# A convolution and softmax-feed-forward kernel: weights converted in PSUM tiles of their own, other load order, g on GpSimd, a second chunk of 16 tokens, four parts in groups 16 to 28

## The chip, the cores and the metric

The kernel runs on one core of a Trainium2 chip. The metric is the device time of one execution in microseconds, lower is better; the figure before is the median of three executions. The profile is of one further execution.

## The reference

Two steps, 8 x 4160 tokens of width 192. First a causal convolution with 7 taps whose weights are a softmax of their own for each token and each of 8 heads; then a feed-forward layer of width 1024 with an activation h * softmax(h), a layer norm over the 1024 values, and a second product.

```python
w = softmax(weight_gen, axis=-1)                      # (8, 4160, 8 heads, 7 taps)
a[b, s, h, :] = sum_k w[b, s, h, k] * x_pad[b, s + k, h, :]   # x_pad: 6 zeros before
h = a @ w_in                                          # (33280, 192) @ (192, 1024)
solu = h * softmax(h)
ln = (solu - mean) / sqrt(var + 1e-6) * g_ln
out = ln @ w_out                                      # (33280, 1024) @ (1024, 192)
```

`x`, `weight_gen` and `g_ln` arrive as float32, `w_in` and `w_out` as float64, and the kernel reads the latter as pairs of 32-bit words.

## The kernel before, in words

**Tiles and groups.** Each of the 128 partitions holds a run of 260 consecutive tokens, so "token t" is a tile of 128 rows, and there are 260 such tiles. x and the taps come in chunks that begin at tokens 0, 4, 12, 20, 36, ... (`starts`, L42). The tiles of x are two buffers (`xt`), used in turn. Within a chunk the convolution works in groups: of two tokens up to token 8, of four afterwards.

**One token.** For a group GpSimd makes the 7 products of x and taps (`attA`, L180), then adds them pairwise until a number of parts is left (`attB`, L195). With the flag True the parts are added by TensorE as it transposes them (`xT`, L474: three transposes of 128x128 for each part and each pair of tokens, accumulated in `pa`); with False VectorE adds them first (`fin`, L458) and one set of transposes follows. After token 16 the groups go through `PARTS`: 3 True, 2 False, 3 True, 3 False; `FIRST` overrules this for early groups. ScalarE and VectorE make a high and a low f16 half of it (`xhi` L484, `xld` L488), and a DMA swaps row halves (`sw`, L494). TensorE makes h in three f16 products (`mm1`, L508 and L513); odd tokens use a second copy of the weights whose rows are swapped (`w0`, `w1`, L290 to L294, DMAs). Then, for each h tile of 128x1024 in PSUM: VectorE scales it and takes its extreme (`max`, L525), ScalarE the exponential (`exp`, L531), VectorE the product (`solu`, L539), ScalarE the squares (`sq`, L545) and the high half (`hi`, L552), VectorE the low half (`lo`, L556), a transposing DMA turns both (`tr`, L564), TensorE makes the second product (`mm2`, L604), ScalarE scales it into `ot` (`out`, L615), and a DMA stores four tokens (`od`, L618). The layer norm's factors are made by small operations for 2 or 4 tokens together (`f0` to `f5`).

**Rings.** h has three PSUM buffers, `po` one. The three h buffers first serve as scratch for the weights, then tokens 0 to 3, then two tiles `c0` and `c1` of the centred second weights, then tokens 4, 5, ... So token 3 waits until token 0's `sq` and `lo` are done, and token 4 for those of token 3.

**The weights.** The words of a double are joined into a float32 by VectorE in PSUM (step 0: L256 once, L260 twice), ScalarE makes a square that tells tiny values (step 1: L266), VectorE multiplies (step 2: L270). `a0`, `a1` and `b` are the first weights, `c0` and `c1` the second. a0 and a1 share one scratch tile, b shares one with c0, c1 has one. The squares of the first weights are summed (`n0` to `n2`, L311), over partitions by TensorE (`n4`, L318), and give the factor `unit_w` (`n6` L322 to L325, `n7` L327), with which the f16 halves are made (`a03` and `a13` L334, `b3` L300 on ScalarE, `a04`, `a14` L336 and `b4` L302 on VectorE). The second weights, kept in the unused end of `xs[1]`, are multiplied by g on ScalarE, eight calls (`q00` to `q30`, L365), summed by TensorE (L370) and ScalarE (L375), centred (`p3`, L388) and split (`p7` L406, `p8` L411).

**Order.** The engines take their instructions in order. The order is made by `plan`, a list of steps with an engine, a cost and what each waits for, and by `issue_order`, which walks through them: the engine that is free takes, of the steps that are ready by the costs, the one with the lowest key. The key is the token's number plus an entry in the table `URGENCY`, by the step's name or by its name and token.

```python
        tile_of, first, n = key
        ...
            bits = bits_of[key] = scratch[tile_of][:, first : first + n].bitcast(I32)
```

Of the kernel before, what the change touches and what calls it, by code (L numbers as in the profile page):

```python
# [26 lines left out]
def tile_kernel(ctx: ExitStack, tc: tile.TileContext, x, weight_gen, w_in, w_out, g_ln, out):  # L27
    nc = tc.nc
# [13 lines left out]
    starts = [0, TG, TG + TC // 2, *range(TG + TC, RUN + 1, TC)]  # L42
# [204 lines left out]
    def float_of_double(key, raw, step, out=None):  # L247

        tile_of, first, n = key
        low = window(raw, 0, [(2, n)])  # L250
        high = window(raw, 1, [(2, n)])
        if step == 0:
            for which in range(len(scratch), 3):
                scratch[which] = ps_h.tile([P, FF], F32, name="h")
            bits = bits_of[key] = scratch[tile_of][:, first : first + n].bitcast(I32)
# [7 lines left out]
        elif step == 1:  # L263
            wide = n > FH
            size = size_of[key] = big.tile([P, n], F32, name="e" if wide else "size")
# [42 lines left out]
    def norm_of_first(step):  # L308
# [6 lines left out]
        elif step == 4:  # L315
            first["total"] = ps_o.tile([P, 512], F32, name="po")
# [34 lines left out]
    def convert(f, step):  # L351
        if step == 2 and "w2" not in second:
            second["w2"] = xs[1].rearrange("p (t d) -> p t d", d=D)[:, -NJ:]
        key = ((1, FH, FH), (2, 0, FF))[f]
        out = None
        if step == 2:
            out = second["w2"].rearrange("p j d -> p (j d)")[:, f * FH : f * FH + key[2]]
        float_of_double(key, raw[3 + f], step, out)
# [71 lines left out]
    def stat_group(t):  # L430

        n = 2 if t < 2 * TG else TG
        return n if t % n == n - 1 else 0
# [163 lines left out]
    def second_product(t):  # L597
        hlT = hlT_of.pop(t)

        free = t >= RUN - TG and t % 2 == 1  # L600
# [16 lines left out]
    def store(t):  # L617
        nc.sync.dma_start(o_run[:, t - TG + 1 : t + 1, :], o_of.pop(t // TG))  # L618
# [54 lines left out]
    a00=79.1, a01=227.6, a02=-179.6, a03=77, a04=-12.8, a10=2, a11=-93.6, a12=123.9, a13=124.9,  # L673
    a14=-132.6, attA=42.9, attA_0=-139.3, attA_2=38.7, attA_4=-121.9, attA_6=101.7, attA_8=-218.2,
    attB=39.9, attB_0=-162.5, attB_2=-4.3, attB_4=74.8, attB_6=-6.9, attB_8=38, b0=133.1, b1=124.8,
    b2=-185.2, b3=24.4, b4=6.5, c00=-95.6, c01=-188.7, c02=-219.3, c10=-222.3, c11=130.7, c12=-70.5,
    c20=-32.3, c21=-46.1, c22=-89, c30=95.7, c31=-78.4, c32=-191, dup=57.3, dup_0=0.9, dup_2=-49.2,
    dup_4=18.3, dup_6=109.3, dup_8=-102.8, exp=-62.2, exp_0=-133.3, exp_1=-123.8, exp_10=41,
    exp_11=-48.7, exp_2=130, exp_3=117.3, exp_4=-23.5, exp_5=-229.6, exp_6=143.2, exp_7=-6.5,
    exp_8=-204.3, exp_9=-18.4, f0=-44.8, f0_1=204, f0_11=72.8, f0_3=17.5, f0_5=17.9, f0_7=216.7,  # L680
    f1=-76, f1_1=20.8, f1_11=-49, f1_3=225.5, f1_5=239.7, f1_7=-14.9, f2=-157.8, f2_1=-115.4,
    f2_11=-19.4, f2_3=230.5, f2_5=-82.5, f2_7=-212.3, f3=34.7, f3_1=-22.7, f3_11=-9.5, f3_3=-53.7,
    f3_5=-121.9, f3_7=-4.3, f4=-58.5, f4_1=167.1, f4_11=69.9, f4_3=-149.7, f4_5=-211.4, f4_7=-100.7,
    f5=-113, f5_1=-19.9, f5_11=23.1, f5_3=75.1, f5_5=47.8, f5_7=96.3, fin=117.5, hi=-107.7,
    hi_0=83.5, hi_1=117.9, hi_10=-193.7, hi_11=86.1, hi_2=-36.8, hi_3=165.8, hi_4=-85.5, hi_5=32.6,
    hi_6=-10, hi_7=-26.8, hi_8=154.8, hi_9=166, lo=-80.2, lo_0=57.7, lo_1=-5.6, lo_10=102.5,
    lo_11=-17.3765, lo_2=-76.7, lo_3=23.7, lo_4=164.3, lo_5=95.8, lo_6=-169.7, lo_7=50, lo_8=-126.6,
    lo_9=75, lw=235.7, lx0=-56.1, lx1=92.4, lx2=8.2, lx3=54.9, max=202.4, max_0=-105.2, max_1=98.3,
    max_10=233.7, max_11=125.3, max_2=-23.8, max_3=200.8, max_4=-205, max_5=-32.1, max_6=149.3,
    max_7=-60.8, max_8=-133.6, max_9=-98.2, mm1=-25.2, mm1_0=-8.9, mm1_1=-9.6, mm1_10=239.3,  # L690
    mm1_11=96.5, mm1_2=158.9, mm1_3=48.1, mm1_4=130.2, mm1_5=-233.5, mm1_6=-5.2, mm1_7=-0.8,
    mm1_8=-2.4, mm1_9=50.4, mm2=-18.3, mm2_0=-4.1, mm2_1=-79.4, mm2_10=182.9, mm2_11=-132.6,
    mm2_2=-211.7, mm2_3=118.1, mm2_4=-93, mm2_5=-224.9, mm2_6=147, mm2_7=10.4, mm2_8=71.6,
    mm2_9=96.2, n0=-12.3, n1=122.3, n2=213.8, n3=-82.1, n4=-104.5, n5=-87.1, n6=-157.4, n7=-151.2,
    nq=-111.6, od=-89.4, od_11=20.6, od_3=16.1, od_7=25.3, out=-192.5, out_0=82.9, out_1=-156.2,
    out_10=54, out_11=-146.8, out_2=232.1, out_3=-56.4, out_4=-28.7, out_5=6.1, out_6=-127.6,
    out_7=23.7, out_8=-74.6, out_9=81.9, p30=-18.7, p31=-152.9, p4=235.2, p5=33.4, p6=-71.9,
    p70=197.2, p71=64.7, p80=-220.6, p81=-108.5, p9=116.9, q00=125.4, q01=-132, q02=161.9,
    q10=219.6, q11=-64, q12=-61.2, q20=206.5, q21=-15.5, q22=-201.1, q30=39.3, q31=0.6, q32=-134.4,
    solu=125.9, solu_0=20.8, solu_1=-3.5, solu_10=129.7, solu_11=17.6, solu_2=6.1, solu_3=-139.9,  # L700
    solu_4=-75.7, solu_5=-145.2, solu_6=161.6, solu_7=-195.9, solu_8=-29.1, solu_9=37.3, sq=-43.8,
# [12 lines left out]
    xld_10=99.8, xld_2=-77.8, xld_4=-238.1, xld_6=8.8, xld_8=133.1,
# [8 lines left out]
FIRST = {0: (7, True), 2: (7, True), 4: (5, True), 6: (5, True), 8: (4, True), 12: (4, True)}  # L723
# [3 lines left out]
def plan(run, starts, group, stat_group, loads, parts):  # L727
# [13 lines left out]
    weights = dict(a0=6600, a1=9300, b=10800, c0=13000, c1=16000)  # L741
    order = list(weights)
    for n, part in enumerate(order):
        at, wide = weights[part], part == "c1"
        once(part + "0", DVE, 3600 if wide else 2050, *([order[n - 1] + "0"] if n else []), ready=at)
        after = [order[n - 1] + "1"] if n else []
        once(part + "1", ACT, 1050 if wide else 620, *after, *([order[n - 2] + "2"] if n > 1 else []), ready=at)
        after = [part + "0", part + "1"]
        if n == 4:
            after.append(order[n - 1] + "2")  # L750
        once(part + "2", DVE, 1220 if wide else 700, *after)
# [6 lines left out]
    for f, part in enumerate(("c0", "c1", "c1", "c1")):  # L758
        once(f"q{f}0", ACT, 770, part + "2", ready=16000)
        once(f"q{f}1", PE, 660, f"q{f}0", *([f"q{f - 1}1"] if f else ["n6"]))  # L760
        once(f"q{f}2", ACT, 520, f"q{f}0", "c12", "n4")
# [25 lines left out]
    for c in range(len(starts) - 1):  # L787
        t, before = starts[c], starts[c - 1] if c > 1 else -1
        size = starts[c + 1] - t
        if c > 1:  # L790
            add("lw", t, SP, 1270, last_group(c - 3))
            add("lx0", t, SP, 1540, last_group(c - 2), *norms(c - 2), *([("p81", 0)] if c == 3 else []))
            for n in range(1, loads):
                add(f"lx{n}", t, SP, 1540, (f"lx{n - 1}", t))
        for n, (name, _) in enumerate(norms(c)):
            if c == 0:
                add(name, t, ACT, (1030, 1260)[n], ready=(7800, 6600)[n])
            else:
                load = [(f"lx{min(n + 1, loads - 1) if size == 16 else loads - 1}", t)] if c > 1 else []
                add(name, t, ACT, 840, *load, ready=18500 if c == 1 else 0)  # L800
# [239 lines left out]
```

## Time and profile before

| | |
|---|---|
| median of 3 executions | 1252.67 us (1252.61 to 1254.92) |
| the profiled execution | 1254.43 us, its span 1252.4 us |
| busy: PE / DVE / ACT / POOL | 1189.2 / 1157.0 / 1128.8 / 1145.7 us |
| instructions | 27,348 |

PE is TensorE, DVE is VectorE, ACT is ScalarE, POOL is GpSimd, SP issues the DMAs. An engine's time before an instruction stands in square brackets behind a row, with what ended it. PEclk is the clock granted to TensorE, as a share of its upper level of 2.4 GHz; 0.50 is its lower level, 1.2 GHz.

### The profile page before, as it was taken

To read this page: it belongs to the slowest core of one execution; us is meant where nothing else is said; L and a number is where in the kernel's file an instruction comes from. 1 tells how busy PE (TensorE), PEld (TensorE's weight loads), DVE (VectorE), ACT (ScalarE), POOL (GpSimd) and SP (SyncE) were. 2 spreads that over 40 slices of the span, in tenths; PEclk is the share of its full clock that TensorE was granted. 3 is DMA by queue.
4 is the path that set the end of the run, shared out by engine and by line. 5 is a ranking of instruction groups with operands and counts; after the bars stand their busy time and mean duration, and the time that the engine had idled before them with its cause. 6 is when DMAs were issued, how large, how long until landed. Compare 5 with 4: busy or idle time off the path is not lost.

```text
span 1252.4 us, 27348 instructions
## 1 busy us (share of the span) xinstructions
PE 1189.2 (95%) x10248; PEld 818.3 (65%) x10248; DVE 1157.0 (92%) x1786; ACT 1128.8 (90%) x2311; POOL 1145.7 (91%) x237
## 2 busy tenths in 40 slices
PE   2598899999999999999999999999999999999997
PEld 2365566666666666666666666666666666666666
DVE  6677999999999999999999999999999999999984
ACT  5778889898998989899998989999898989989886
POOL 5899999999999999999999999999999999999400
PEclk9799999999999999999999999999999999999999
DMA  7577688897989999798989989798988979877667
GB/s 222 112 189 172 132 190 168 192 197 144 213 169 198 176 183 199 149 213 165 212 166 181 184 170 213 152 208 166 202 164 191 199 145 198 167 148 149 139 140 139
DMA packets 586066, 219.75 MB, mean 175 GB/s; under 512 B 548687, under 2 KB 566223, under 8 KB 585806
## 3 DMA queue, kind: packets, MB, share of 16 engines
q1 hardware_dynamic: 585632, 216.91, 84.6%
q8 instruction: 80, 1.31, 0.4%
q10 hardware_dynamic: 302, 1.11, 0.3%
q14 instruction: 52, 0.43, 0.1%
HBM read 46.19 MB, written 25.56 MB: 57 GB/s over the span
## 4 chain that ended last, share of the span: by engine, by line
PE 34%; ACT 33%; DVE 17%; issue 11%; DMA 4%; SPq 0%; ACTq 0%; DVEq 0%
PE po L604 13%; PE h L513 11%; ACT e L531 9%; ACT e L545 8%; ACT hl L552 6%; PE h L508 6%; DVE h L539 5%; DVE h L525 4%; DVE a L458 4%; PE pa L474 3%; DVE hl L556 3%; ACT junk L145 3%; ACT ot L615 2%; DMA hlT<-hl 2%; ACT xh L484 2%
## 5 line engine op out<-in xcount | busy, mean ns | idle before, releaser
L180 POOL TENSOR_TENSOR pr<-xt,wt 128x5376 f32<-128x5376 f32 (+1 forms) x67 | 631.1, 9420 | 0.2
L604 PE MATMUL po<-w_hl,hlT 128*128 128x192 f16 x6192 | 554.1, 247 | 8.7 <-DMA hlT<-hl 4.5
L604 PEld LDWEIGHTS <-hlT 128*128 128x128 f16 x6240 | 523.1, 98 | 52.9 <-issue 6.0
L195 POOL TENSOR_TENSOR pr<-pr 128x2304 f32<-128x2304 f32 (+1 forms) x126 | 458.3, 3637 | 7.6
L556 DVE SCALAR_TENSOR_TENSOR hl<-h,hl 128x1024 f16<-128x1024 f32 x260 | 314.6, 1220 | 41.5 <-ACT e L545 26.4
L525 DVE TENSOR_SCALAR_CACHE_REDUCE h<-h,row 128x1024 f32<-128x1024 f32 x260 | 334.8, 1288 | 12.9 <-PE h L513 8.7
L539 DVE SCALAR_TENSOR_TENSOR h<-h,row,e 128x1024 f32<-128x1024 f32 x260 | 333.3, 1282 | 10.3 <-ACT e L531 7.6
L531 ACT ACTIVATE e<-h,stats 128x1024 f32<-128x1024 f32 x260 | 292.9, 1126 | 15.1 <-DVE h L525 14.4
L552 ACT ACTIVATE hl<-h 128x1024 f16<-128x1024 f32 x260 | 266.4, 1025 | 36.7 <-DVE h L539 18.5
L545 ACT ACTIVATE e<-h,stats 128x1024 f32<-128x1024 f32 x260 | 292.2, 1124 | 2.6 <-DVE h L539 2.0
L513 PEld LDWEIGHTS <-xh 128*128 128x128 f16 x1560 | 131.9, 98 | 236.5 <-issue 115.0
L513 PE MATMUL h<-w_odd,xh 128*128 128x512 f16 x780 | 192.7, 384 | 0.0
L513 PE MATMUL h<-wa_hi,xh 128*128 128x512 f16 x520 | 178.4, 384 | 0.0
L615 ACT ACTIVATE ot<-po,stats 128x192 f32<-128x192 f32 x258 | 110.5, 428 | 36.4 <-PE po L604 36.0
L508 PE MATMUL h<-w_odd,turned 64*128 64x512 f16 x390 | 107.4, 382 | 10.7 <-DVE hl L556 10.1
L508 PE MATMUL h<-wb_hi,xh 64*128 64x512 f16 x260 | 99.9, 384 | 14.6 <-DVE hl L556 12.5
L508 PE MATMUL h<-w_odd,xh 64*128 64x512 f16 x390 | 107.6, 383 | 0.0
L508 PE MATMUL h<-wb_hi,turned 64*128 64x512 f16 x260 | 100.1, 385 | 0.0
L513 PE MATMUL h<-wa_lo,xh 128*128 128x512 f16 x260 | 99.2, 381 | 0.0
L508 PEld LDWEIGHTS <-xh 64*128 64x128 f16 x780 | 54.7, 94 | 54.8 <-issue 26.0
L474 PE MATMUL pa<-ident,pr 128*128 128x128 f32 x678 | 87.7, 277 | 0.6 <-DVE xh L488 0.6
L474 PEld LDWEIGHTS pa<-ident,pr 128*128 128x128 f32 x678 | 78.6, 144 | 7.9 <-DVE xh L488 1.1
(89 smaller groups left out, 1020.4 us busy)
## 6 DMA issues: line engine op xcount, KB each, us to landing
out_dram<-ot SPq DMA_DIRECT2D x65, 384.0 KB, 3.5
xt<-in_x_dram SPq DMA_DIRECT2D x30, 576.0 KB, 5.0
xt<-in_x_dram SPq DMA_DIRECT2D x30, 480.0 KB, 4.3
turned<-xh SPq DMA_DIRECT2D x260, 32.0 KB, 2.6
wt<-in_weight_gen_dram SPq DMA_DIRECT2D x15, 448.0 KB, 4.8
hlT<-hl SPq DMA_TRANSPOSE x260, 4.6
xt<-in_x_dram SPq DMA_DIRECT2D x3, 384.0 KB, 4.4
pr<-in_moe_w_out_dram SPq DMA_DIRECT2D x1, 1024.0 KB, 10.3
```

The source lines that it names most:

```text
L180: nc.gpsimd.tensor_tensor(out=window(pr, 0, [(ROW, K), (HG, n * H), (1, HG)]), in0=window(xt, t * D, [(D, K), (HG, n * H), (1, HG)]), in1= ...
L195: nc.gpsimd.tensor_tensor(out=b, in0=b, in1=a, op=ALU.add)
L474: nc.tensor.matmul(pa[:, k], source[:, first : first + P], ident, is_transpose=True, start=at == 0, stop=at == 3 * len(sources) - 1,)
L508: nc.tensor.matmul(h[:, fs], last[(f + odd) % 2][rows, low], rhs[rows], start=n == 0, stop=False)
L513: nc.tensor.matmul(h[:, fs], xh[:, 2 * odd, low], rhs[:, fs], start=False, stop=n == 2)
L525: nc.vector.tensor_scalar(h, h, row(t, BACK), 3.0e38, op0=ALU.mult, op1=ALU.min, accum_out=stat(t, NMAX))
L531: nc.scalar.activation(e, h_of[t], AF.Exp, bias=stat(t, NMAX), scale=-1.0, accum_out=stat(t, Z))
L539: nc.vector.scalar_tensor_tensor(out=h, in0=h, scalar=row(t, SCALE), in1=e, op0=ALU.mult, op1=ALU.mult, accum_out=stat(t, M))
L545: nc.scalar.activation(e_of.pop(t), h_of[t], AF.Square, bias=stat(t, M), scale=-float(FF), accum_out=stat(t, Q),)
L552: nc.scalar.activation(hl[:, 0, :], h_of[t], AF.Copy, scale=2.0**14)
L556: nc.vector.scalar_tensor_tensor(out=hl[:, 1, :], in0=h_of[t], scalar=2.0**14, in1=hl[:, 0, :], op0=ALU.mult, op1=ALU.subtract,)
L604: nc.tensor.matmul(po[:, :D], hlT[:, half * NJ + j, :], w2_hl[:, j, w, :], start=n == 0, stop=n == len(terms) - 1,)
```

## The change

- The chunks begin at 0, 4, 20, 36, ...: one chunk of 16 tokens in place of two of 8. The second weights lie at the end of `xs[0]` now, whose next load, of the chunk at token 20, waits for them.
- x of the first chunk is loaded behind all of `w_in`: on SP's queue behind `raw[2]`, and its six tokens of halo on ACT's queue behind `raw[1]`.
- a0, a1 and b have a scratch tile each; the second weights become three pieces of 512 (c0, c1, c2) that go through the single `po` buffer one after the other. The sum of the first weights' squares goes into b's tile.
- g is applied by GpSimd, one instruction of 128x384 for each of four parts, in place of eight on ScalarE.
- Groups 16, 20, 24 and 28 have four parts, all added by TensorE.
- The factors of the layer norm are made for four tokens together from the start.
- At the end, odd tokens from 255 on (before: from 257 on) put the second product into an h buffer, and the last token is stored by itself, behind a store of three.
- The table `URGENCY` is a new one, and the planner lets transposes count as work that keeps the clock up.

```diff
-    starts = [0, TG, TG + TC // 2, *range(TG + TC, RUN + 1, TC)]
+    starts = [0, *range(TG, RUN + 1, TC)]
     nc.sync.dma_start(raw[0], w_in[:P, :FF])
-    load_x(0)
     nc.scalar.dma_start(raw[1], w_in[:P, FF:])
     for f in range(2):
         nc.sync.dma_start(raw[2][f * D2 : (f + 1) * D2, :], w_in[P:, f * FF : (f + 1) * FF])
+    load_x(0)
...
+            if tile_of == 3:
+                scratch[3] = ps_o.tile([P, 512], F32, name="po")
-            bits = bits_of[key] = scratch[tile_of][:, first : first + n].bitcast(I32)
+            bits = bits_of[key] = scratch[tile_of][:, :n].bitcast(I32)
-            first["b"] = float_of_double((1, 0, FH), raw[2], step)
+            first["b"] = float_of_double((2, 0, FH), raw[2], step)
-            first["total"] = ps_o.tile([P, 512], F32, name="po")
+            first["total"] = scratch[2][:, FH : FH + 8]
-            first[f] = float_of_double((0, f * FH, FH), raw[f], step)
+            first[f] = float_of_double((f, 0, FH), raw[f], step)
-            second["w2"] = xs[1].rearrange("p (t d) -> p t d", d=D)[:, -NJ:]
-        key = ((1, FH, FH), (2, 0, FF))[f]
+            second["w2"] = xs[0].rearrange("p (t d) -> p t d", d=D)[:, -NJ:]
+        key = (3, f * FH, FH)
+        words = (raw[3], raw[4][:, : 2 * FH], raw[4][:, 2 * FH : 4 * FH])[f]
-            for j in range(j0, j1):
-                nc.scalar.activation(w2[:, j, :], w2[:, j, :], AF.Copy, scale=g[:, j : j + 1])
+            nc.gpsimd.tensor_tensor(
+                out=w2[:, j0:j1], in0=w2[:, j0:j1],
+                in1=g[:, j0:j1].unsqueeze(2).broadcast_to([P, JP, D]), op=ALU.mult,
+            )
-        n = 2 if t < 2 * TG else TG
-        return n if t % n == n - 1 else 0
+        return TG if t % TG == TG - 1 else 0
-        free = t >= RUN - TG and t % 2 == 1
+        free = t >= RUN - 6 and t % 2 == 1
-        nc.sync.dma_start(o_run[:, t - TG + 1 : t + 1, :], o_of.pop(t // TG))
+        t0 = RUN - 1 if t == RUN - 1 else t - t % TG
+        nc.sync.dma_start(o_run[:, t0 : t + 1, :], o_of[t // TG][:, t0 % TG : t % TG + 1, :])
-FIRST = {0: (7, True), 2: (7, True), 4: (5, True), 6: (5, True), 8: (4, True), 12: (4, True)}
+FIRST = {0: (7, True), 2: (7, True), 4: (5, True), 6: (5, True), 8: (4, True), 12: (4, True), 16: (4, True), 20: (4, True), 24: (4, True), 28: (4, True)}
...
```

## Rows read from the trace of the kernel before

**Rows 1.** Busy time of each engine in four stretches of 50 us and one of 10 us (columns: stretch and its length, then for PE, PEld, DVE, ACT and POOL the busy time and the number of instructions, then the granted clock, the DMA share and GB/s).

```profile
0.00:50.00 50.00, 25.18 (x132) 17.89 (x133) 31.69 (x56) 30.06 (x79) 29.84 (x19) 0.93 0.62 183
50.00:100.00 50.00, 37.59 (x314) 26.30 (x313) 37.95 (x66) 41.61 (x98) 49.69 (x10) 0.86 0.72 170
100.00:150.00 50.00, 39.90 (x293) 23.61 (x291) 42.59 (x65) 42.38 (x87) 49.69 (x11) 0.93 0.70 142
150.00:200.00 50.00, 49.31 (x430) 33.94 (x431) 47.76 (x71) 45.20 (x89) 49.69 (x11) 1.00 0.89 187
...
10.00:20.00 10.00, 1.18 (x4) 1.01 (x4) 7.44 (x13) 7.11 (x17) 5.77 (x4) 1.00 1.04 349
```

**Rows 2.** The timeline, weights: start, duration, engine, line, operation, in square brackets the idle time before it.

```profile
7.37 0.69 DVE L256 TENSOR_SCALAR h<-hlT 128x512 int32<-128x512 int32 x1 [0.56 <-DMA hlT<-in_moe_w_in_dram]
8.10 1.42 DVE L260 SCALAR_TENSOR_TENSOR h<-hlT,h 128x512 int32<-128x512 int32 x2
11.19 0.84 ACT L145 ACTIVATE junk<-xt 128x768 f32<-128x768 f32 x1 [3.18 <-DMA xt<-in_x_dram]
12.15 0.16 DVE L151 TENSOR_REDUCE row<-squares_x 128x1 f32<-128x8 f32 x1 [2.63 <-ACT junk L145]
18.80 0.70 DVE L270 SCALAR_TENSOR_TENSOR h<-size,h 128x512 f32<-128x512 f32 x1
21.78 0.60 ACT L311 ACTIVATE junk<-h 128x512 f32<-128x512 f32 x1 [2.38 <-DVE h L260]
22.97 4.63 PE L474 MATMUL pa<-ident,pr 128*128 128x128 f32 x21
28.02 0.80 ACT L365 ACTIVATE xt<-xt,g 128x192 f32<-128x192 f32 x2
```

**Rows 3.** DMA issues of the first 40 us: what, queue, count, KB each, median us from issue to landing.

```profile
xt<-in_x_dram SPq DMA_DIRECT2D x1, 768.0 KB, 8.6
hlT<-in_moe_w_in_dram ACTq DMA_DIRECT2D x1, 512.0 KB, 10.1
xt<-in_x_dram ACTq DMA_DIRECT2D x1, 504.0 KB, 4.7
```

**Rows 4.** The timeline, from the last DMA of the swapped weights to the first second product.

```profile
37.82 0.59 SPq L294 DMA_DIRECT2D w_odd<-wa_lo  x1
36.91 1.28 DVE L525 TENSOR_SCALAR_CACHE_REDUCE h<-h,row 128x1024 f32<-128x1024 f32 x1
41.05 0.61 PE L508 MATMUL h<-w_odd,turned 64*128 64x512 f16 x1
46.14 1.22 DVE L556 SCALAR_TENSOR_TENSOR hl<-h,hl 128x1024 f16<-128x1024 f32 x1
62.88 1.22 DVE L556 SCALAR_TENSOR_TENSOR hl<-h,hl 128x1024 f16<-128x1024 f32 x1
64.25 0.58 PE L508 MATMUL h<-wb_hi,xh 64*128 64x512 f16 x1 [11.77 <-DVE hl L556]
68.18 2.23 PE L604 MATMUL po<-w_hl,hlT 128*128 128x192 f16 x24
```

**Rows 5.** The timeline of GpSimd.

```profile
16.99 9.84 POOL L180 TENSOR_TENSOR pr<-xt,wt 128x2688 f32<-128x2688 f32 x2
35.75 0.97 POOL L124 TENSOR_TENSOR wt<-wt,wy 128x448 f32<-128x448 f32 x1 [8.91 <-DVE row L165]
36.79 4.94 POOL L180 TENSOR_TENSOR pr<-xt,wt 128x2688 f32<-128x2688 f32 x1
41.81 1.81 POOL L195 TENSOR_TENSOR pr<-pr 128x768 f32<-128x768 f32 x1
100.24 1.75 POOL L124 TENSOR_TENSOR wt<-wt,wy 128x896 f32<-128x896 f32 x1
1166.55 6.96 POOL L195 TENSOR_TENSOR pr<-pr 128x2304 f32<-128x2304 f32 x2
```

**Rows 6.** The timeline of TensorE and VectorE: transposes of 7, 4 and 3 parts (21, 12 and 9 of them), a second product, and a sum by VectorE.

```profile
29.30 2.46 PE L474 MATMUL pa<-ident,pr 128*128 128x128 f32 x21
90.19 1.47 PE L474 MATMUL pa<-ident,pr 128*128 128x128 f32 x12
103.23 1.15 PE L474 MATMUL pa<-ident,pr 128*128 128x128 f32 x9
118.47 3.04 PE L604 MATMUL po<-w_hl,hlT 128*128 128x192 f16 x24 [3.58 <-DMA hlT<-hl]
128.86 1.77 DVE L458 TENSOR_REDUCE a<-pr 128x768 f32<-128x1536 f32 x1
```

**Rows 7.** The timeline of the end.

```profile
1237.89 2.14 PE L604 MATMUL po<-w_hl,hlT 128*128 128x192 f16 x24 [0.51 <-ACT ot L615]
1240.54 2.14 PE L604 MATMUL po<-w_hl,hlT 128*128 128x192 f16 x24 [0.51 <-ACT ot L615]
1241.17 2.06 SPq L564 DMA_TRANSPOSE hlT<-hl  x1
1246.48 2.15 PE L604 MATMUL h<-w_hl,hlT 128*128 128x192 f16 x24
1249.11 0.33 SPq L618 DMA_DIRECT2D out_dram<-ot  x1
```

**Rows 8.** The page's DMA issues, the transposing one: queue, count, median us from issue to landing.

```profile
hlT<-hl SPq DMA_TRANSPOSE x260, 4.6
```

More of the change, by code (lines that the diff above doesn't have):

```diff
@@ L263, in float_of_double @@
         elif step == 1:
-            wide = n > FH
-            size = size_of[key] = big.tile([P, n], F32, name="e" if wide else "size")
+            size = size_of[key] = big.tile([P, n], F32, name="size")
             nc.scalar.activation(size, high.bitcast(F32), AF.Square)
@@ L643, in tile_kernel @@
     for n in range(3):
-        for f in range(2):
+        for f in range(3):
             ops[f"c{f}{n}"] = once(convert, f, n)
@@ L684 @@
[L684 to L689, printed above, removed]
@@ L739, in chunk_of @@
         return max(c for c in range(len(starts) - 1) if starts[c] <= t)
-    weights = dict(a0=6600, a1=9300, b=10800, c0=13000, c1=16000)
+    weights = dict(a0=7000, a1=9300, b=10500, c0=14400, c1=17400, c2=17400)
     order = list(weights)
     for n, part in enumerate(order):
-        at, wide = weights[part], part == "c1"
-        once(part + "0", DVE, 3600 if wide else 2050, *([order[n - 1] + "0"] if n else []), ready=at)
+        at = weights[part]
+        once(part + "0", DVE, 2150, *([order[n - 1] + ("2" if n > 3 else "0")] if n else []), ready=at)
         after = [order[n - 1] + "1"] if n else []
-        once(part + "1", ACT, 1050 if wide else 620, *after, *([order[n - 2] + "2"] if n > 1 else []), ready=at)
+        once(part + "1", ACT, 620, *after, *([order[n - 2] + "2"] if n > 1 else []), ready=at)
         after = [part + "0", part + "1"]
-        if n == 4:
+        if n > 3:
             after.append(order[n - 1] + "2")
-        once(part + "2", DVE, 1220 if wide else 700, *after)
+        once(part + "2", DVE, 700, *after)
         if n < 3:
@@ L757, in plan @@
     once("w1", SP, 2500, "a04", "a14", "b4")
[L758 to L761, printed above, removed]
+    for f, part in enumerate(("c0", "c1", "c2", "c2")):
+        once(f"q{f}0", POOL, 780, part + "2", ready=16000)
+        once(f"q{f}1", PE, 660, f"q{f}0", *([f"q{f - 1}1"] if f else ["c22"]))
+        once(f"q{f}2", ACT, 520, f"q{f}0", "n4")
     for half, old in enumerate(centred_after()):
@@ L796, in plan @@
             if c == 0:
-                add(name, t, ACT, (1030, 1260)[n], ready=(7800, 6600)[n])
+                add(name, t, ACT, (1030, 1260)[n], ready=(11500, 10500)[n])
             else:
                 load = [(f"lx{min(n + 1, loads - 1) if size == 16 else loads - 1}", t)] if c > 1 else []
-                add(name, t, ACT, 840, *load, ready=18500 if c == 1 else 0)
+                add(name, t, ACT, 840, *load, ready=(19500 + 700 * n) if c == 1 else 0)
         add("v1", t, DVE, 74, *norms(c), *norms(c - 1), ("f5", starts[c - 4] - 1 if c > 4 else -1))
@@ L837, in plan @@
         if i == 2:
-            after += [("c10", 0), ("c11", 0)]
+            after += [("c10", 0), ("c11", 0), ("c20", 0), ("c21", 0)]
         if i > 2:
             after += consumers(groups[i - 3])
-        add("attA", t, POOL, 30 + 9690 * size, *after, ready=19000 if c == 1 else 0)
+        add("attA", t, POOL, 30 + 9690 * size, *after, ready=22300 if c == 1 else 0)
         adds = 7 - count
@@ L894, in plan @@
             add("f5", t, DVE, 75, ("f4", t))
-        if t % 4 == 3:
-            add("od", t, SP, 1092, ("out", t))
+        if t % 4 == 3 or t == run - 2:
+            add("od", t, SP, 1092 if t < run - 1 else 300, ("out", t))
     return steps
@@ L904, in readers @@
 def readers(u):
-    scratch = (["a04", "a14"], ["b4", "c02"], ["c12"])
+    scratch = (["a04"], ["a14"], ["b4", "n6"])
     if isinstance(u, str):
@@ L982, in issue_order @@
         if e == PE:
-            if name != "xT" and time - busy > 2000:
+            if time - busy > 2000:
                 warm = time + 3400
@@ L987, in issue_order @@
                 free[e] = end = time + 2 * cost if time + 2 * cost < warm else (time + warm) / 2 + cost
-            if name != "xT":
-                busy = end
+            busy = end
         if e == SP:
```

89 lines of the change are left out of this document (48 added, 41 removed).

## The prediction

> **What bounds the kernel now.** I read first the busy time in stretches [rows 1]. From 150 us on TensorE is busy over 98% of the time (49.31 of 50) at full clock, so there the end is set by TensorE's work and nothing that only shortens another engine is worth anything. Before 150 us it is idle for 24.8 + 12.4 + 10.1 = 47.3 us, and in the same stretches the clock averages 0.93, 0.86 and 0.93: with the busy times that is 25.2 x 0.07 + 37.6 x 0.14 + 39.9 x 0.07 = 9.8 us more. So about 57 us can be won at the start, and whatever TensorE's work is brought forward there arrives at the end in full, if no other engine then becomes the bound. GpSimd is full too (49.69 of 50) from 50 us on, but its last row ends at 1173.5 us [rows 5], some 75 us before the end: it runs ahead.
>
> Next the timeline of the start, backwards from the longest hole. Token 4 begins at 64.25 after 11.77 us of idleness, released by VectorE's `lo` of token 3, which gives its h buffer back [rows 4]. Token 3 hangs in the same way on `lo` of token 0 (46.14), token 1 begins only at 41.05, behind the swapped weights, whose last DMA is issued at 37.82. Those hang on the f16 weights, these on the factor `unit_w`, this on the squares of b, which start at 21.78 after 2.38 us of waiting for a L260 of VectorE [rows 2]. That L260 belongs to c0, not to b (b's last step is at 18.80): c0 and b lie in one scratch tile. And VectorE stood for 2.63 us before 12.15 because its next instruction in order was the sum for x [rows 2], with the second half of `w_in` landing at the same time (issued at 1.9 on ACT's queue behind the halo of x, 10.1 us to landing [rows 3]).
>
> **The change part by part.**
>
> *Load order and scratch tiles.* With `w_in` ahead of x on both queues, `raw[1]` no longer lands at 12.0, and VectorE can go from a0 (7.37 + 0.69 + 1.42 = 9.5) to a1 and b without a hole: 2.6 us. With tiles of its own b's square no longer waits for c0: 2.4 us. And c0's first three instructions (2.1 us) need no longer be ahead of anything of b. b is done at 7.4 + 3 x 2.1 + 3 x 0.7 = 15.8 us in place of 19.5, its square at 16.5 in place of 22.4, so `unit_w` comes some 6 us earlier. What is late next: x of chunk 0. The halo now lies behind `raw[1]`, so I put its landing at about 11 (before: 4.7 us after its issue [rows 3]) and x at about 12 (before: 11.1 [rows 2]); GpSimd's multiplication of the halo then ends near 15 and the first products start at 16 to 17 as before (16.99 [rows 5]). So token 0 stays where it is, 31.7, minus at most the 1 us by which its transposes (22.97) stand behind the matmuls of the factor. Token 1 does not: the last DMA of its swapped weights is issued some 8 us sooner than 37.82 (unit_w's 6 and part of the copies by g below), so it follows token 0 at 33 to 34 instead of 41.05.
>
> *g on GpSimd.* Eight calls of 0.4 us leave ACT (0.80 for two [rows 2], so 3.2 us), which from 28 on stood in front of the halves and the constants of chunk 1. On GpSimd four instructions of 384 elements: the nearest row is 1.81 us for 768, so 0.9 each, 3.6 us, within the 8.91 us in which GpSimd waits before 35.75 [rows 5]. Free with that cover, 3.6 us later for every group without it.
>
> *One chunk of 16.* Its load is 1536 KB instead of 768 (8.6 us to landing [rows 3]); at the 349 GB/s of the stretch from 10 to 20 us [rows 1] 2.3 us later, near 22.5. Four squares of 0.84 [rows 2] instead of two, the constants, and two GpSimd instructions of 1.75 (896 elements) instead of 0.97 (448) [rows 5] follow. I put the products of token 4 at 31 to 33 instead of 36.79. The same work of the chunk at 12 disappears around 54 to 61 us, where ACT was the busiest. The three pieces c0 to c2 in one `po` buffer cost nothing on VectorE (it is in order anyway), but TensorE's sums start only after c2; they are needed for the second product at 68 us only [rows 4].
>
> *The sum for token 4.* Token 1 is 7 to 8 us earlier; `max` of token 0 (36.91, three us after its product) can follow at 33; `lo` of token 0 (46.14) comes near 41, token 3 near 42 instead of 48.6. From token 3 to its `lo` it took 14 us, with two squares and the constants of the chunk at 12 inside: 13 now. Token 4 at about 55 instead of 64.25: **-9 us**. Bounds: 0 if a new wait takes the place, -14 if the whole hole of 11.77 goes and token 0 comes 2 us earlier.
>
> *Four parts.* Twelve transposes take 1.47, nine 1.15 [rows 6]: 0.32 for a part and pair. Groups 16 to 28 had 3, 1, 3, 1 sets: eight more, for two pairs each, 16 x 0.32 = 5.2 us of TensorE. GpSimd saves 1 + 2 + 1 + 1 sums of 1.81 us [rows 5], which is worth nothing while it is ahead; VectorE saves two L458 (1.77 for two parts [rows 6], by that 2.66 for three), the first of which stands on the path of token 20. Half of the transposes (groups 16 and 20) fall where TensorE idles 10 us in 50, half where it is full. I take **+2.6**, bounds 0 and +5.2, and **-1.7** for the L458 (0 to -4.4).
>
> *Clock.* The first 21 transposes took 4.63 us, the next 21, after little else than transposes, 2.46 [rows 2, 6]: so transposes here came to run at the upper level. The price if the added 48 ran as the first 21 did: 48 x (4.63 - 2.46) / 21 = 5.0 us, the fourth rival. The Trainium skill ("TensorE: Matmul & The Clock Gate", "Part 4: PE-mode transpose") says that transposes do not count as work for the clock in the way matmuls do; the two rows speak against it.
>
> *Order anew.* The holes of 64 to 150 us, such as the 3.58 for a transposing DMA before 118.47 [rows 6], come from the order. I cannot bound a new one from below by rows except by the holes that there are (12 us); I take 0, bounds -8 and +8.
>
> *The end.* Two waits of 0.51 for `po` go with 255 in an h buffer [rows 7]. The last product (1246.48) can come only 0.7 us earlier, as its transposing DMA, issued at 1241.17, lands 4.6 us later [rows 8], at 1245.8. The last store carries a quarter of the bytes; its 384 KB, issued at 1249.11 [rows 7], took 3.3 us to the end of the span, so I take 0.5 off. **-1.2**, bounds 0 and -2.
>
> Sum: -9 + 2.6 - 1.7 + 0 - 1.2 = -9.3. Against the profiled execution's 1254.43: 1245.1. It was 1.8 us above the median of the three runs, so for the median the same sum would give 1243.4; I keep **1245**, the more cautious one.
>
> **The rivals.**
>
> 1. *The gain is given back.* From 64 to 150 us VectorE and ACT are 76 to 85% busy, each token's chain goes through both several times, and three h buffers allow no more. If these set the pace until TensorE is full, the work arrives no earlier; then only the end (-1.2) and part of the transposes (+2.6) remain, less what is left of -9, say -2: 1253.8. For it: TensorE was hardly ever waiting for GpSimd. Against: those engines start earlier as well, and 4.4 us of VectorE's work are gone.
>
> 2. *GpSimd starves TensorE: slower.* If GpSimd, in order, waits for c2 or for the longer load of chunk 4 with the products of token 4 behind it, these begin later than 36.79. Group 16 was ready at 100.24 [rows 5] and transposed at 103.23 [rows 6]: 3.0 us to spare, 4.8 with its one sum less. The decisive point is a start of token 4's products later than 41.6. At 45 group 16 comes at 100.24 + 8.2 - 1.8 = 106.6, the head's gain is gone, and 3.4 + 5.2 - 1.2 = +7.4 remain: 1261.8; at 42, 1258.8. I take 1260. Against: a hole of 8.91 us precedes it now.
>
> 3. *The change doesn't do what it says.* If the square of b still waits (for instance because the sum of squares lies in b's tile and is tracked as one), or the halo of x is so late that token 0 slips, half the head's gain remains: -4.5 in place of -9, 1249.6.
>
> 4. *Transposes at the lower clock.* The 48 cost 5.0 more: 1250.1.
>
> **How the numbers follow.** Forecast 0.58, rivals 0.14, 0.13, 0.11 and 0.04. What a measurement can tell from no change is about 0.2%, 2.5 us: faster is below 1250.2, slower above 1255.2. The forecast's own range is 1236 (head -14, order -4) to 1250. Faster: 0.57 of the forecast, 0.07 of rival 3, 0.02 of rival 4, 0.01 of rival 1: 0.67. Same: 0.11 of rival 1, 0.04 of rival 3, 0.02 of rival 4 and 0.01 of the forecast: 0.18. Slower: rival 2 and 0.02 of rival 1: 0.15. The range to hold it 8 times in 10 is 1236 to 1254.
>
> **What would show it.** In the new profile: b's square (L311) without a wait for L260 and near 17 us; token 1's product within 3 us of token 0's; token 4's before 58; no L365-like row on ACT and four of about 0.9 us on GpSimd; products of token 4 before 35; TensorE's busy time of 100 to 150 us above 43. Wrong would be the forecast if TensorE's hole before token 4 stays over 8 us, if the stretch of 100 to 150 shows as much idleness as before with VectorE or ACT as its cause, or if a GpSimd product (L180) releases TensorE.

## The result: slower by 0.7%, with a start that won more than forecast

| | before | after |
|---|---|---|
| median | 1252.67 us | 1261.43 us |
| lowest to highest of five executions | 1251.77 to 1254.92 | 1257.49 to 1266.31 |
| ratio after to before | | 1.0069 [1.0051, 1.0087] |
| the profiled execution, its span | 1254.43, 1252.4 us | 1261.43, 1259.7 us |

The forecast was 1245 us and a range of 1236 to 1254: too low, and on the wrong side of no change. Engine busy times by stretches of 50 us, the view of [rows 1], of the kernel after (columns as there):

```profile
0.00:50.00 50.00, 23.57 (x144) 16.90 (x144) 37.58 (x66) 33.45 (x82) 36.43 (x23) 1.00 0.61 186
50.00:100.00 50.00, 45.46 (x363) 30.68 (x364) 41.52 (x64) 41.79 (x87) 49.69 (x9) 0.93 0.80 170
100.00:150.00 50.00, 47.87 (x401) 32.02 (x399) 46.53 (x76) 47.26 (x98) 49.92 (x9) 1.00 0.83 178
150.00:200.00 50.00, 49.53 (x435) 33.96 (x434) 45.10 (x70) 47.09 (x96) 49.61 (x11) 1.00 0.86 196
...
250.00:300.00 50.00, 46.88 (x395) 31.95 (x394) 44.55 (x69) 43.37 (x93) 49.77 (x11) 0.97 0.85 153
```

TensorE is idle for 26.4 + 4.5 + 2.1 = 33.0 us before 150 us, against 47.3. The start has 14 us of idleness less. But in a stretch where the prediction held TensorE's work for the bound it now stands still for 3.1 us of 50, at a mean clock of 0.97. The same view in two stretches, first the second one before:

```profile
200.00:1180.00 980.00, 972.39 (x8485) 669.35 (x8484) 945.39 (x1452) 914.64 (x1857) 966.84 (x190) 1.00 0.89 179
```

and both after:

```profile
0.00:200.00 200.00, 166.43 (x1337) 113.56 (x1338) 170.73 (x273) 169.59 (x360) 185.65 (x49) 0.98 0.78 183
200.00:1180.00 980.00, 957.92 (x8288) 653.70 (x8287) 925.95 (x1419) 895.92 (x1815) 954.62 (x187) 1.00 0.86 175
```

The number of matmuls tells the loss: 8288 instead of 8485 in the same 980 us, 197 fewer. At 8485 / 980 = 8.66 per us that is 22.8 us of work. By the diff no part of the change but the new order touches the work of this stretch (h1 below tests it). What each engine waits for in it, in total, how many times and the longest, is in the waits of 200 to 1200 us after:

```profile
ACT hl L555 <- DMA hlT<-hl: 21.9, 12, 3.5
...
PE po L607 <- ACT ot L618: 15.1, 11, 3.0
...
POOL wt L124 <- DVE wy L122: 16.4, 9, 4.0
```

and, the same lines of code, before:

```profile
ACT hl L552 <- DMA hlT<-hl: 0.9, 1, 0.9
PE po L604 <- ACT ot L615: 0.5, 1, 0.5
```

Two waits have grown, from one time each: ScalarE's `hi` for the transposing DMA, twelve times, and TensorE's second product for ScalarE's `out`, eleven times. GpSimd's for VectorE, nine times, has no row before. How the first makes the second is in the timeline of after around 250 us (of its rows those of this chain):

```profile
242.93 2.44 DVE L559 SCALAR_TENSOR_TENSOR hl<-h,hl 128x1024 f16<-128x1024 f32 x2
...
245.55 4.17 SPq L497 DMA_DIRECT2D turned<-xh  x2
...
249.82 5.56 SPq L567 DMA_TRANSPOSE hlT<-hl  x2
...
255.25 1.02 ACT L555 ACTIVATE hl<-h 128x1024 f16<-128x1024 f32 x1 [3.51 <-DMA hlT<-hl]
256.30 1.23 DVE L559 SCALAR_TENSOR_TENSOR hl<-h,hl 128x1024 f16<-128x1024 f32 x1 [3.44 <-ACT hl L555]
257.54 0.41 ACT L618 ACTIVATE ot<-po,stats 128x192 f32<-128x192 f32 x1
258.01 3.46 PE L607 MATMUL po<-w_hl,hlT 128*128 128x192 f16 x24 [3.04 <-ACT ot L618]
```

Read it from below. The second product of 258.01 needs the one `po` buffer, which `out` gives back at 257.95. `out` stands behind `hi` in ScalarE's order, and `hi` waits 3.51 us: `hl` has three buffers, and the one that it wants is still read by a transposing DMA: the first of the two in the row of 249.82, although its `lo`, the first of the two in the row of 242.93, had ended by 244.15. SP's queue had other work in front: loads of x, a store and, from 245.55 on, two swaps (4.17 us). ScalarE's in-order queue thus carries a late DMA to TensorE. The clock adds to it: of 250 to 260 us the granted mean is 0.87, and from 258 to 260 it is 0.50, the lower level of 1.2 GHz, after TensorE had stood for 3.04 us; the product takes 3.46 us instead of the 2.14 of its neighbours. It comes back every 16 tokens (in one turn of ten without a wait); the next such row and three later ones in ScalarE's timeline after:

```profile
329.46 1.02 ACT L555 ACTIVATE hl<-h 128x1024 f16<-128x1024 f32 x1 [1.46 <-DMA hlT<-hl]
...
844.52 1.02 ACT L555 ACTIVATE hl<-h 128x1024 f16<-128x1024 f32 x1 [2.53 <-DMA hlT<-hl]
919.02 1.02 ACT L555 ACTIVATE hl<-h 128x1024 f16<-128x1024 f32 x1 [1.45 <-DMA hlT<-hl]
992.53 1.02 ACT L555 ACTIVATE hl<-h 128x1024 f16<-128x1024 f32 x1 [1.78 <-DMA hlT<-hl]
```

Ten turns of 16 tokens take 992.53 - 255.25 = 737.3 us, 73.7 each. This reading is a theory until a run removes the wait and the time goes with it.

The start, in the timeline after, for the prediction's steps [rows 2, 4, 5]:

```profile
9.58 0.69 DVE L258 TENSOR_SCALAR h<-hlT 128x512 int32<-128x512 int32 x1 [2.46 <-DMA hlT<-in_moe_w_in_dram]
14.66 3.20 POOL L239 TENSOR_SCALAR xt<-xt,inside 128x1152 f32<-128x1152 f32 x1 [8.37 <-ACT junk L145]
19.16 0.60 ACT L312 ACTIVATE junk<-h 128x512 f32<-128x512 f32 x1 [0.42 <-DVE h L271]
20.20 4.94 POOL L180 TENSOR_TENSOR pr<-xt,wt 128x2688 f32<-128x2688 f32 x1
25.20 4.17 PE L477 MATMUL pa<-ident,pr 128*128 128x128 f32 x21 [3.86 <-POOL pr L180]
30.79 2.40 POOL L366 TENSOR_TENSOR xt<-xt,g 128x384 f32<-128x384 f32 x3
30.89 2.51 PE L477 MATMUL pa<-ident,pr 128*128 128x128 f32 x21 [0.42 <-POOL pr L180]
34.09 0.39 PE L511 MATMUL h<-wb_hi,xh 64*128 64x512 f16 x1
34.98 4.94 POOL L180 TENSOR_TENSOR pr<-xt,wt 128x2688 f32<-128x2688 f32 x1
38.41 0.39 PE L511 MATMUL h<-w_odd,turned 64*128 64x512 f16 x1
50.24 0.87 PE L477 MATMUL pa<-ident,pr 128*128 128x128 f32 x6 [2.27 <-POOL pr L195]
54.22 0.58 PE L511 MATMUL h<-wb_hi,xh 64*128 64x512 f16 x1 [3.10 <-DVE w_hl L415]
```

Token 4 begins at 54.22 (before 64.25, forecast 55), with 3.10 us of idleness ahead of it instead of 11.77. GpSimd's first products come 3.2 us later than before. They and one of its sums release TensorE's transposes (3.86, 0.42 and 2.27 us of waiting); before, TensorE's waits between 20 and 300 us have no row for GpSimd.

### The profile page after: what moved, and what is told of

It reads as the page before. It is cut to its first block, busy times and chain, and to the rows that moved or that the text cites. A ratio compares the mean times of both kernels' runs of the same rounds, so it can differ in the third digit from the quotient of the medians.

```text
span 1259.7 us, 27355 instructions
## 1 busy us (share of the span) xinstructions
PE 1196.3 (95%) x10296; PEld 820.8 (65%) x10296; DVE 1151.4 (91%) x1777; ACT 1124.0 (89%) x2286; POOL 1140.3 (91%) x235
## 4 chain that ended last, share of the span: by engine, by line
ACT 31%; PE 25%; DVE 21%; issue 13%; DMA 8%; POOL 1%; ACTq 0%; SPq 0%; DVEq 0%; POOLq 0%
PE po L607 9%; ACT hl L555 9%; ACT e L534 9%; PE h L516 7%; ACT e L548 7%; DMA hlT<-hl 7%; DVE h L542 6%; DVE hl L559 6%; PE h L511 4%; DVE h L528 4%; DVE a L461 4%; PE pa L477 3%; ACT ot L618 2%; ACT stats L594 1%; ACT junk L145 1%
## 5 line engine op out<-in xcount | busy, mean ns | idle before, releaser
L195 POOL TENSOR_TENSOR pr<-pr 128x2304 f32<-128x2304 f32 (+1 forms) x122 | 449.6, 3686 | 7.3
L477 PE MATMUL pa<-ident,pr 128*128 128x128 f32 x738 | 94.7, 276 | 6.6 <-POOL pr L180 4.3
L477 PEld LDWEIGHTS pa<-ident,pr 128*128 128x128 f32 x738 | 84.5, 143 | 14.4 <-POOL pr L180 5.2
L511 PEld LDWEIGHTS <-turned 64*128 64x128 f16 x780 | 54.2, 94 | 43.6 <-issue 23.8
```

What stands on the lines that cost most here:

```text
L195: nc.gpsimd.tensor_tensor(out=b, in0=b, in1=a, op=ALU.add)
L477: nc.tensor.matmul(pa[:, k], source[:, first : first + P], ident, is_transpose=True, start=at == 0, stop=at == 3 * len(sources) - 1,)
L511: nc.tensor.matmul(h[:, fs], last[(f + odd) % 2][rows, low], rhs[rows], start=n == 0, stop=False)
```

## The experiments

Every ratio is to the kernel before, run beside it. "A" is the theory that the new order of the long middle costs more than the start wins; the rivals are in the expectations.

**Keys of before in the order of after, and the reverse.** The entries of `URGENCY` without a token number govern the middle. Four runs replace them: all of them in after (e1), all of them in before (e2), in after only those of SP's steps (e3) and only those of ScalarE's steps (e4). One line of e3 as an example:

```diff
-    sq_5=20.8, sq_6=76.5, sq_7=-91.5, sq_8=243.3, sq_9=135.1, sw=184.3, sw_0=150, sw_10=2.4,
+    sq_5=20.8, sq_6=76.5, sq_7=-91.5, sq_8=243.3, sq_9=135.1, sw=-185.3, sw_0=150, sw_10=2.4,
```

> The changed kernel, but the table's entries for steps that come back with every token, group or chunk (the names without a token's number, which hold from token 12 on) are those of before. Theory A (the start is some 15 us better, and the new order of the long middle loses some 1.6 us in every 16 tokens, 23 us in all): the middle goes back to 72.0 us for 16 tokens and the time is about 1238, at most 1245. Theory B (the middle is slowed by another part of the change: the chunk of 16, the four parts or GpSimd's earlier start, which shift the phases against each other): still 1256 to 1264, with waits of ACT's hi for the transposing DMA. Theory C (half and half): 1246 to 1252.

> The kernel before, with the changed kernel's entries for those steps. Theory A: the middle loses, 1268 to 1278, and ACT's hi waits for the transposing DMA once in 16 tokens. Theory B: within 3 us of before, 1250 to 1256. Theory C: 1258 to 1266.

> The changed kernel with only the entries of SP's steps (sw, tr, od, lw, lx0 to lx3) as before. If theory A holds and the place of the swapping DMA ahead of the transposing one in SP's queue is the cause (A1): most of the loss goes, 1238 to 1248, and the waits of ACT's hi for the DMA fall from 21.9 us below 6. If ACT's own order, hi ahead of the others, is the cause (A2): 1256 to 1264 with those waits as they are.

> The changed kernel with only the entries of ACT's steps (exp, sq, hi, out, xhi, f0, f2, f4, t2, t4, v00 to v03, v2, v3, v5) as before. A1: still 1256 to 1264. A2: 1238 to 1248, and TensorE's second product no longer waits for out (15.1 us between 200 and 1200).

Measured: e1 1281.91 us, 1.0227 [1.0212, 1.0243]; e2 1329.38, 1.0597 [1.0577, 1.0618]; e3 1289.35, 1.029 [1.0271, 1.0309]; e4 1279.79, 1.0205 [1.019, 1.0221]. All four are slower than both kernels and outside every range expected of them, so they tell nothing for or against A: a table of keys is one solution, and half of another makes an order that neither kernel has.

**The finished orders joined.** Here the two orders are made whole and cut at the first product of token 40. h1: after up to there, then the order of before (and its end). h2: the reverse.

```diff
+    later = [x for x in others[others.index(("mm1", 40)) :] if x in set(mine)]
+    joined = [x for x in mine if x not in set(later)] + later
```

> Not the keys but the finished orders are joined: every step up to the place of token 40's first product comes in the changed kernel's order, every later one in the order of before; the code of all steps is the changed one's, but the end (h buffers for odd tokens, the last store) is that of before. Theory A (the new order of the middle is the loss): the middle runs at 72.0 us for 16 tokens and the 15 us of the start stay: 1236 to 1243. Theory B (the middle of the changed kernel is slow because of the other changes, whatever the order): 1256 to 1266.

> The other way round: code and order of before up to token 40, then the changed kernel's order and its end. Theory A: the middle takes some 73.6 us for 16 tokens, 1270 to 1280. Theory B: 1250 to 1256.

h1 1240.67 us, 0.9898 [0.9879, 0.9918]; h2 1279.27, 1.0211 [1.018, 1.0241]. So the start of after is worth some 12.5 us (h1 against the 1253.12 of before beside it), and the middle of after costs 1261.43 - 1240.67 = 20.8 behind its own start, 26.2 behind that of before. h2 also has the two waits:

```profile
ACT hl L552 <- DMA hlT<-hl: 20.4, 11, 3.2
PE po L604 <- ACT ot L615: 14.6, 12, 2.6
```

A holds. Open was what in the order costs it.

**The swap behind the transposing DMA.** In the hole above the two swaps stand ahead of the late transposing DMA. e5 moves the swap, each 16 tokens.

```diff
+    for t in range(48, RUN, TC):
+        sw, tr = order.index(("sw", t)), order.index(("tr", t - 7))
+        if sw < tr:
+            order.insert(tr, order.pop(sw))
```

> The changed kernel with one thing moved in its finished order: for t = 48, 64, ... 256 the swapping DMA of token t is issued behind the transposing DMA of token t - 7 instead of ahead of it. Theory A1 (this place in SP's queue makes hi of token t - 4 wait for the DMA, ACT stands with it, the scaling of the second product comes late and TensorE stands): the 12 waits of hi for the DMA (21.9 us) go to below 5, TensorE's waits for out (15.1 us between 200 and 1200) below 4, and the time falls to 1244 to 1250. Theory A2 (ACT's or VectorE's order is the cause and the DMA only ends the wait last): 1257 to 1264.

1259.36 us, 1.0047 [1.0029, 1.0065]: 2 us less than after, within the scatter of both (1252.36 to 1262.14 here), and the waits that A1 saw go are there. A row of its timeline, and then two of its waits, say why:

```profile
244.94 6.73 SPq L567 DMA_TRANSPOSE hlT<-hl  x1
```

```profile
ACT hl L555 <- DMA hlT<-hl: 19.9, 12, 2.8
...
PE po L607 <- ACT ot L618: 12.0, 11, 2.1
```

The transposing DMA is next on SP's queue now, from 244.94 on, and takes 6.73 us to issue. So the swap's place is not the cause; what SP's queue waits for in these 6.73 us the profile does not name.

**One engine's finished order at a time.** From token 40 on e6 takes SP's order from before and the rest from after, e7 the orders of TensorE, VectorE and ScalarE from before and those of SP and GpSimd from after (the last argument, here e6's, names the engines).

```diff
-    for op, t in issue_order(plan(RUN, starts, group, stat_group, LOADS, parts)):
+    joined = merged(steps, mine, middle, (3,))
+    for op, t in joined:
```

> The changed kernel; from token 40 on SP issues its DMAs in the finished order of before, all other engines keep the changed kernel's order. Theory A1 (SP's order is the loss: in the new one three large transfers and the swap stand between two transposing DMAs): 1238 to 1246, hi's waits for the DMA gone. Theory A2 (the order on ACT, VectorE and TensorE is the loss, the DMA only ends the wait last): 1255 to 1264.

> The reverse: from token 40 on TensorE, VectorE and ACT take the finished order of before, SP and GpSimd keep the changed kernel's. A1: 1253 to 1264. A2: 1238 to 1246.

e6 1296.11 us, 1.0344 [1.0326, 1.0363]; e7 1307.03, 1.0431 [1.0413, 1.0449]. Both are outside all the ranges expected of them. Orders that were not made for each other cost more here than the loss itself, so whether one engine's order carries the loss these two runs cannot tell.

**A fourth `hl` buffer.** Theory M: the cost is the wait of `hi` for a buffer, wherever the lateness of the DMA comes from. e8 leaves the order of after as it is and gives `hl` a buffer more; the space comes from `size`, which now lies in the buffers of `e`.

```diff
-            size = size_of[key] = big.tile([P, n], F32, name="size")
+            size = size_of[key] = big.tile([P, FF], F32, name="e")[:, :n]
...
-        hl = hl_of[t] = big.tile([P, 2, FF], F16, name="hl", bufs=3)
+        hl = hl_of[t] = big.tile([P, 2, FF], F16, name="hl", bufs=4)
```

> The changed kernel, its order untouched, with four buffers for the two halves (hl) instead of three; the room comes from putting the square of the weights' conversion (size) into the e buffers. The high half of token t then waits for the transposing DMA of token t - 4 instead of t - 3. Theory M (that wait, 21.9 us of ACT between 200 and 1200, is what the new order runs into, and through the late scaling it stops TensorE): the 12 waits vanish and the time is 1244 to 1250. Rival N (the DMA only ends a wait that ACT's order would have anyway, the loss lies in how the engines' orders interlock): 1256 to 1264.

1238.25 us (1238.16 to 1238.37), 0.9883 [0.9867, 0.99]: 23.2 us less than after, below both kernels and below the 1244 to 1250 that M gave. In its waits of 200 to 1200 us `hi` has no row for the DMA any more, GpSimd none for VectorE, and of TensorE's for `out` this is left:

```profile
PE po L607 <- ACT ot L618: 0.5, 1, 0.5
```

Its middle by stretches:

```profile
200.00:1180.00 980.00, 974.82 (x8485) 666.49 (x8484) 945.60 (x1452) 917.98 (x1854) 954.42 (x187) 1.00 0.88 178
```

and the place of the hole in its timeline:

```profile
246.52 7.76 SPq L567 DMA_TRANSPOSE hlT<-hl  x2
...
251.51 1.02 ACT L555 ACTIVATE hl<-h 128x1024 f16<-128x1024 f32 x1
...
253.89 0.41 ACT L618 ACTIVATE ot<-po,stats 128x192 f32<-128x192 f32 x1
...
254.69 2.14 PE L607 MATMUL po<-w_hl,hlT 128*128 128x192 f16 x24
...
970.77 1.02 ACT L555 ACTIVATE hl<-h 128x1024 f16<-128x1024 f32 x1
```

The two transposing DMAs still take 7.76 us on the queue, but `hi` begins at 251.51 without a wait, the product at 254.69 and at its full speed. The matmuls of the stretch are 8485 again, as before the change. Ten turns take 970.77 - 251.51 = 719.3 us, 71.9 each: 1.8 less than in after, and 1.8 x 980 / 73.7 = 24 us over the stretch. Three controls: c1 is both edits in before, c2 both in h1, c3 the first alone in after.

> The kernel before with four hl buffers and size in the e buffers. If the fourth buffer only takes away the wait that the new order runs into: 1251 to 1255, since ACT waits for the transposing DMA only once (0.9 us) in before. If a fourth buffer is worth something to any order: 1240 to 1248.

> The joined kernel (start of the changed one, middle and end of before, 1240.7) with four hl buffers. If its middle is already bound by TensorE: 1239 to 1242. If the changed kernel's own middle with four buffers (1238.3) is the better order: 1240 or more here, so 1238.3 stays the best.

> The changed kernel with three hl buffers as it is, and only size in the e buffers, the edit that made room for the fourth. If the fourth buffer is the cause of the 1238.3: 1256 to 1264 with hi's waits for the DMA as before. If the moved size were it: 1238 to 1246.

c1: 1251.9 us, 0.9995 [0.9985, 1.0005], worth nothing, since that order has the wait once (0.9 us). c2: 1239.06, 0.989 [0.9873, 0.9908], what e8 has: with four buffers the two orders of the middle take the same time. c3: 1264.76, 1.0091 [1.0059, 1.0124], 0.8 above its range; that edit is not what helps. c3's waits, in the window of the others, are longer than those of after, and so is its time:

```profile
ACT hl L555 <- DMA hlT<-hl: 27.7, 13, 3.2
...
PE po L607 <- ACT ot L618: 20.0, 12, 2.6
```

M is shown, and the wait for the buffer is the whole of the loss, not a part as M's range had it.

**The end.** h3 is h1 with the end of after from the first product of token 236 on.

> The changed kernel in full, its own order up to token 40 and from token 236 on, the order of before between. If the end of the change brings the 1.2 us that were forecast for it: 1238 to 1241 (the joined one with the end of before took 1240.7). If it brings nothing or the joint costs: 1240 to 1244.

1242.55 us, 0.9914 [0.9899, 0.9929], against 0.9898 for h1: the new end wins nothing that can be measured.

**The parts of the start, one undone at a time.** All four stand on h3, with its order kept: p1 has three parts in groups 16 to 28, p2 loads x of chunk 0 where before did, p3 shares the scratch tiles as before did, p4 applies g on ScalarE. The order was made for the kernel with all four, so a difference holds for this order.

```diff
@@ p1 @@
+        if 16 <= t <= 28:
+            return 3, True
@@ p2 @@
     nc.sync.dma_start(raw[0], w_in[:P, :FF])
+    load_x(0)
...
-    load_x(0)
@@ p3 @@
-            first["b"] = float_of_double((2, 0, FH), raw[2], step)
+            first["b"] = float_of_double((1, 0, FH), raw[2], step)
...
-            first[f] = float_of_double((f, 0, FH), raw[f], step)
+            first[f] = float_of_double((0, f * FH, FH), raw[f], step)
...
-        key = (3, f * FH, FH)
+        key = ((1, FH, FH), (2, 0, FH), (2, FH, FH))[f]
@@ p4 @@
-            nc.gpsimd.tensor_tensor(
...
+            for j in range(j0, j1):
+                nc.scalar.activation(w2[:, j, :], w2[:, j, :], AF.Copy, scale=g[:, j : j + 1])
```

> h3 with three parts (added by TensorE) instead of four in groups 16 to 28, the order kept: TensorE has 8 x 0.32 = 2.6 us less, GpSimd four sums of 1.8 us more. If GpSimd is ahead there, as the forecast had it: 2 to 3 us faster than h3. If the start of the changed kernel has made GpSimd the bound (its products released TensorE in the start): 1 to 6 us slower than h3.

> h3 (changed kernel, order of before between tokens 40 and 236; 1242.6) with x of the first chunk loaded between the two halves of w_in again, as before; order kept. By the forecast's step (a hole of 2.6 us on VectorE) 2 to 4 us slower than h3. If the first products on GpSimd set the start, which come earlier with an earlier x: 1 to 3 us faster.

> h3 with the scratch tiles of before: a0 and a1 in one, b with c0, c1 and c2 in one, the sum of squares in the po buffer; order kept. By the forecast's step (b's square waits for c0) 1 to 3 us slower than h3. If in the new order b's square is issued ahead of c0 anyway: within 1 us of h3.

> h3 with g applied on ScalarE again, eight calls, at the same places of the order. By the forecast (3.2 us of ACT in front of the halves, covered on GpSimd): 1 to 4 us slower than h3. If GpSimd is the bound from its first product of token 4 on: up to 3 us faster, as 3.2 us leave GpSimd.

p1 1248.99 us, 0.9963 [0.995, 0.9975]: 6.4 slower than h3. p2 1241.62, 0.9909 [0.9894, 0.9924], and p4 1242.49, 0.9917 [0.9903, 0.9932]: no difference, where the forecast's step gave 2 to 4 and 1 to 4 slower. p3 1245.27, 0.994 [0.9925, 0.9955]: 2.7 slower. p1 is the surprise. Waits for GpSimd's sums from 20 to 300 us, h3:

```profile
PE pa L477 <- POOL pr L195: 2.3, 1, 2.3
```

and p1, with three parts and so one sum more in each of these groups:

```profile
PE pa L485 <- POOL pr L195: 8.0, 8, 2.3
```

Seven of the eight lie between 117 and 243 us. And of p3, ScalarE's squares of a0 and of b:

```profile
15.33 0.60 ACT L310 ACTIVATE junk<-h 128x512 f32<-128x512 f32 x1 [3.97 <-DVE h L260]
...
21.37 0.60 ACT L310 ACTIVATE junk<-h 128x512 f32<-128x512 f32 x1 [0.20 <-DVE h L269]
```

and of p2, VectorE's first step of a1:

```profile
12.71 0.69 DVE L258 TENSOR_SCALAR h<-hlT 128x512 int32<-128x512 int32 x1 [2.37 <-DMA hlT<-in_moe_w_in_dram]
```

## Why the prediction was wrong

**The step that failed is "Order anew: I take 0, bounds -8 and +8".** It cost 21 us (after against h1) to 23 (after against e8), almost three times the upper bound, and by itself turns the sign. The bound had been taken from the holes that the old order left, but a new order is not bounded by the old one's holes: a wait that occurs once in before, too small for the prediction to have read it, comes twelve times. The argument from [rows 1], that past 150 us only TensorE's work counts, described one order as if it were the kernel. None of the rivals held this: rival 1 gives the gain back in the start, rival 2 starves TensorE there, and neither looked past 150 us. That rival 2's 1260 lies near the measured time is luck. With the order's cost in place of 0 the sum is 1245.1 + 20.8 = 1265.9, some 4 us above the profiled 1261.43; that rest is the start, won larger than forecast.

**The start.** Forecast: -9 for token 4, +2.6 and -1.7 for the four parts, together -8.1; token 4's own move came out at -10.0 us, and the whole start at some -12.5 (h1, whose end is that of before). By its steps:

- Load order: put at part of the gain, worth about nothing (p2). It moved a wait: VectorE's first step comes at 9.58 instead of 7.37; with x back in its old place (p2) it comes at 7.38, and VectorE waits 2.37 us for `raw[1]` before 12.71. So b's square ends at 19.76, not 16.5. GpSimd's first products come at 20.20, not 16 to 17: its multiplication of the halo (14.66) waits for ScalarE's squares of x, which the new order puts behind the square of a0 (12.59). In p2, with x loaded sooner, the products come at 20.88.
- Scratch tiles: 2.7 us (p3), but not by the wait that the forecast named. In after b's square waits only for its own L271 (0.42 us); in p3, with the tiles shared again, it waits 0.20 us for its own last step too, and not for c0. There a0's square waits 3.97 us for a step of a1, which has the same tile; the squares of x come behind it, and GpSimd's first products start at 22.94 against 21.05 in h3.
- g on GpSimd: its cost there nothing, as put, and 0.80 us each (forecast 0.9). The 3.2 us taken off ScalarE, which the forecast counted for token 1, were worth nothing either (p4).
- Four parts: a gain of 6.4 against three parts (p1). p1 is not the groups of before, of which two were summed by VectorE; by the prediction's prices p1 saves TensorE 8 x 0.32 = 2.6 us and costs nothing, since it put GpSimd's sums of 1.81 at nothing "while it is ahead". With a faster start GpSimd is not ahead: it releases TensorE, and in this order a sum saved there is worth more than the transposes that replace it. Against the groups of before the four parts were not measured.
- Token 0 came at 34.09 (forecast 31 to 31.7), token 1 at 38.41 (33 to 34), and token 4 at 54.22 (55): the tokens begin later and follow one another faster. 12.5 less 2.7 and 6.4 leaves about 3.4 us to the chunk of 16, the factors made for four tokens and the order of the start together, if the parts add. None of these was undone by itself; that stays open.

**Rival 2** had its mechanism right, a GpSimd product releases TensorE, and its price wrong: token 4's products began at 34.98, well before the 41.6 from which it would decide. **Rival 4** did not occur: all the sets of twelve transposes between 69 and 156 us took 1.47 us, as before [rows 6]. **The end**: -1.2 forecast, nothing found (h3). Its waits of 0.51 for `po` are still there at 1238.55 and 1244.47, and 1.13 at 1241.82.

Shown is that `hi` waits for an `hl` buffer because transposing DMAs come late in the new order, that this wait is the loss (e8, c3), and that the old order hardly has it (once in before, 0.9 us; twice in h1, 1.2 us). Not shown is why SP's queue gets behind in just this order.

## What to carry to other kernels

What a faster start wins arrives only if the steady middle keeps pace, so a change that makes the order anew must be priced there first: here 1.8 us lost in each turn of 16 tokens cost 23 us, more than the 12.5 us that the start won. Look in the waits for the row in which a buffer is reused behind a DMA; one buffer more gave 23 us here with the order untouched, as much as going back to the old order of the middle did, and nothing where that row was nearly empty. And a saving on an engine that is "ahead" has a price as soon as the change brings forward what it feeds.

## What was not expected of the hardware

- The first 21 transposes took 4.17 us and the next 21, 1.5 us later, 2.51, as in [rows 2, 6]. Between the two sets TensorE made only four small products, and ahead of the first it had stood for 3.86 us. The granted clock reads 1.00 from 20 to 35 us in both kernels, so that the first set ran at the lower level, as the prediction took it, is not shown. The durations look like it: six such transposes took 1.54 us in e1 (at 50.78) where the granted clock was 0.50, and 0.87 in after (at 50.24) where it was 1.00. The Trainium skill ("TensorE: Matmul & The Clock Gate", "Part 4: PE-mode transpose") says that transposes do not count as work for the clock as matmuls do. If the clock did rise between the two sets, both kernels' traces speak against it for these f32 transposes; the granted clock does not settle it.
- One transposing DMA can hold SP's queue for 6.73 us (e5, while chunk loads are under way); after issued another at 257.03 in 1.79, and the median between 200 and 1200 us is 2.0 in after. The issue itself, not only the landing, has to be planned for.
- The kernel after scatters over 8.8 us in five executions, and e8, in the same order, over 0.2.
